# Retention and gated feed-forward on one core: two chunks' small products put in joint runs in two more places

## The chip, the core and the metric

The kernel runs on one core of a Trainium2 chip, as one program. The metric is device time in microseconds (us). Before the change three runs took 613.05, 612.64 and 612.45 us, a median of 612.64. The profiled execution that all views below come from took 613.15 us; its span from the first to the last instruction is 611.4 us, and the granted TensorE clock is 1.000 over the whole of it.

## The reference

The first half is a retention layer (batch 4, 8 heads, 768 steps, head size 64). The second half is a feed-forward layer over the 3072 resulting rows, with w_in of 512 x 2048 and w_out of 2048 x 512:

```python
for t in range(S):
    state = gamma * state + k_t (outer) v_t
    y[t] = scale * q_t @ state
x = y, as 3072 rows of 512
h = x @ w_in
sp = max(h, 0) + log1p(exp(-|h|))
out = (h * erf(sp)) @ w_out
```

## The kernel before, in words

**Chunks and groups.** The 3072 rows are 24 chunks of 128 steps (six for each batch entry). Two chunks, called a and b below, are a group of 256 rows; there are NG = 12 groups, numbered from 0. The retention of a chunk is computed in half-chunks of 64 steps, in products of 64 x 64 on quarters of TensorE's array, and gives the transposed input x of the feed-forward layer. The group's hidden values h = x @ w_in are computed 128 features at a time ("ft", 16 of them), go to DRAM, and are read back later for softplus, erf, the gate, and the product with w_out.

**The steps of one chunk j.**
- `ret_transpose(j)` (L447, called `T`): for the first six chunks, 4 + 4 transposes of keys and queries on TensorE (128 x 128, L453), copied out of PSUM by ScalarE (L459). Later chunks get theirs from VectorE (`prepare`, L531).
- `scale_early(j, 1)` and `scale_early(j, 0)` (L742): ScalarE scales the queries, then the values, by the decays, eight activations each (L746).
- `begin(j)` (L560): the scores of both half-chunks (L566) and what they add to the state (L573), 64 x 64 products into two PSUM banks.
- `states(j)` (L578): VectorE masks the scores into the tile `am` (L582) and adds up the states (L593).
- `results(j)` (L595): the products with the state (L611) and with the masked scores (L622), into two more banks; ScalarE copies them to x (L630).
- `crossed_sums(j)` (L633) adds a part of the results on VectorE (L641); `split_x` (L643) splits x into the parts hi, lo and dif that the three-product scheme uses (L314 to L316).

The last chunk of a batch entry has one half-chunk less to add to the state, and the first has no state for its first half.

**What sets the order.** The order on every engine is written out by hand: each engine works its queue in the order in which the Python code issues instructions. Three stretches matter here.

*First stretch, groups 0 to 2.* A loop over the 16 ft computes `hidden_of(ft, 0)` and `hidden_of(ft, 1)` (L659, plain f32 products, L665), and after each ft runs the steps that the table `during` (L799) lists for it, then `put_hidden(ft)` (L671): ScalarE copies the two groups' hidden values out of one of two PSUM buffers (L673), and GpSimd's queue stores them (L675). VectorE converts the 64-bit weights to f32 meanwhile (`conversion`, L237, lines L244 to L265), piece by piece, before the ft that needs them. The two chunks of the third group (4 and 5) are worked in here.

*Middle, `period(g)` (L936).* Eight `unit`s or `pair_unit`s (L687, L712) for each group, each 12 products of three-part f32 (L720), beside the chunks of group g + 1. For the groups 3 to 9 `joined(2, 5, g)` (L925) places `begin` of both chunks ahead of unit 2 and `results` of both ahead of unit 5, one right after the other.

*Last group but one, `period(10)`.* `begin(a)` stands ahead of unit 1, `results(a)` ahead of unit 2, `begin(b)` ahead of unit 3, `results(b)` ahead of unit 5. The units of this period go on to load and split w_out, and to start the first softplus.

**Buffers.** `b4` gives one of 34 SBUF buffers of 4 KB a partition, `b2` one of 6 of half that size. The tile `am` of a chunk (masked scores) is a `b2`; so is the tile h of `put_hidden` and of `put`, which is free again only when its store has landed. PSUM tiles come from the pools `ps_r` (2 banks), `ps_h` (2) and the four named banks o0 to o3.

**Tables.** `load_block_scales` (L387) loads small decay tables through GpSimd's queue in the first stretch; `block_scales` (L400) takes their reciprocals on VectorE (L401 to L403) and has GpSimd multiply them up (L405); the first reader is `prepare` of chunk 6 (L538).

Of the kernel before, what the change touches and what calls it, by code (L numbers as in the profile page):

```python
# [23 lines left out]
JPC = 4  # L24
# [25 lines left out]
def kernel(  # L50
# [14 lines left out]
    B, H, S, D = q.shape  # L65
    d_model, d_ff = w_in.shape
    HP = H // 2
# [17 lines left out]
    ps_r = ctx.enter_context(tc.tile_pool(name="ps_r", bufs=2, space=PSUM))  # L85
# [4 lines left out]
    def b4(name, shape, dtype=F32):  # L90
        return big.tile([P] + shape, dtype, name=name, tag="b4")

    def b2(name, shape, dtype=F32):
        return small.tile([P] + shape, dtype, name=name, tag="b2")
# [16 lines left out]
    KN, QN, V, KB, QB, KT, QT, SC, AM, SU = {}, {}, {}, {}, {}, {}, {}, {}, {}, {}  # L111
# [33 lines left out]
    def load_pair(j):  # L145

        b, c = divmod(j, NC)
        KNP[j] = b4("kn", [2, H, D])
        KB[j], QB[j] = (b4(name, [HP, 2 * C]) for name in ("kb", "qb"))
        for i in range(2):  # L150
            load_values(j + i, nc.gpsimd)
            KN[j + i], SLOT[j + i] = KNP[j][:, i], head
            nc.gpsimd.dma_start(KN[j + i], of_chunk(k, j + i))
        yield
        for to, src in ((KB[j], k), (QB[j], q)):
            for s, d in itertools.product(range(2), range(2)):
                part = slice((2 * s + d) * 32, (2 * s + d + 1) * 32)
                for u in range(HP):
                    nc.sync.dma_start(
                        to[part, u].rearrange("p (a d) -> p a d", d=32),  # L160
                        src[b, head(u, s), c * C : (c + 2) * C, d * 32 : (d + 1) * 32].rearrange(
                            "(a p) d -> p a d", p=32
                        ),
                    )
                yield
# [387 lines left out]
    def state_of(j, a):  # L553

        return None if j % NC == 0 and a == 0 else ST[(2 * j + a) % 5]

    def additions(j):
        return range(2 if j % NC < NC - 1 else 1)
# [18 lines left out]

    def states(j):  # L578

        AM[j] = b2("am", [2, HP, D])  # L580
        for s in range(2):
            nc.vector.tensor_tensor(  # L582
                AM[j][:, s],
                SC[j][s][:, :, :D],
                causal_d[:, None, :].to_broadcast([P, HP, D]),
                op=ALU.mult,
            )
        for a in additions(j):
            to, x, new = ST[(2 * j + a + 1) % 5], state_of(j, a), SC[j][a][:, :, D:]
            if x is None:  # L590
                nc.vector.tensor_copy(to, new)
            else:
                nc.vector.tensor_tensor(to, x, new, op=ALU.add)  # L593
# [118 lines left out]
    def pair_unit(g, ft):  # L712
# [23 lines left out]
    Q_, V_, T, S_, M, O_, A = (  # L736
        scale_q, scale_v, ret_transpose, ret_scores, ret_mask, ret_out, ret_add
    )
# [53 lines left out]
    def steps(s, n=1):  # L792
# [3 lines left out]
    pair = load_pair(JPC + 2)  # L796
    prep = prepare(JPC + 2)
    a, b = JPC, JPC + 1
# [1 line left out]
        1: [(load_block_scales,)],  # L800
        2: [(scale_early, a, 1), (steps, pair, 2)],
        3: [(scale_early, a, 0), (T, a, None, ("o2", "o3")), (steps, pair, 2)],
        4: [(begin, a, ps_r), (steps, pair, 2)],
        5: [(scale_early, b, 1), (states, a), (steps, pair, 2)],
        6: [(scale_early, b, 0), (results, a, ("o0", "o1")), (T, b, None, ("o2", "o3")), (steps, pair), (block_scales,)],
        7: [(crossed_sums, a), (begin, b, ps_r), (split_weights, 0)],
        8: [(states, b), (split_weights, 1)],
        9: [(results, b, ("o0", "o1"))],
        10: [(crossed_sums, b), (split_x, a, 2)],
        11: [(steps, prep, 3)],  # L810
        12: [(split_weights, 2), (steps, prep, 1)],
        13: [(steps, prep, 1)],
        14: [(begin, a + 2, ps_r), (begin, b + 2, None, ("o2", "o3")), (split_weights, 3), (states, a + 2), (states, b + 2)],
    }
    for ft in range(n_ft):
# [109 lines left out]
    def joined(at, to, g):  # L925

        a, b = 2 * g + 2, 2 * g + 3
        return {
            at: [(begin, a, ps_h), (begin, b, ps_r)],
            to: [(results, a, None, ps_h), (results, b, None, ps_r)],  # L930
        }
# [4 lines left out]
    def period(g, prep, next_prep):  # L936

        a, b = 2 * g + 2, 2 * g + 3
        one, two = partial(partial, unit), partial(partial, pair_unit)
        if g == G2:  # L940
            units = [one(g, n) for n in range(NPC // 2)]
            return units, {0: [(results, a), (results, b, None, ps_h)]}, {
                0: [(crossed_sums, a), (crossed_sums, b)],
                1: [(split_x, a, 2)],
                2: [(split_weights, 4)],
                3: [(steps, next_prep, 4)],
            }, range(4)
        if g < NG:
            units = [two(g - 1, ft) for ft in range(8 * (g % 2), 8 * (g % 2) + 8)]
        if g == G2 + 1:  # L950
            return units, joined(2, 5, g), {
                0: [(steps, prep)],
                1: [(split_weights, 5)],
                2: [(states, a), (states, b)],
                3: [(split_weights, 6)],
                4: [(split_weights, 7)],
                5: [(crossed_sums, a), (crossed_sums, b)],
                6: [(split_x, a, 2)],
                7: [(steps, next_prep, 1)],
            }, range(4)  # L960
        if g < NG - 2:
            return units, joined(2, 5, g), {
                0: [(steps, prep, 4)],
                1: [(convert, 2)],
                2: [(states, a), (convert, 1)],
                3: [(states, b), (convert, 1)],
                4: [(convert, 2 if g < 8 else 1)],
                5: [(crossed_sums, a), (crossed_sums, b)],
                6: [(split_x, a, 2)],
                7: [(steps, next_prep, 1 if g < NG - 3 else 4), (convert, 1)],  # L970
            }, LOADS.get(g, ())
        if g == NG - 2:
            return units, {1: [(begin, a)], 2: [(results, a)], 3: [(begin, b)], 5: [(results, b)]}, {
                0: [(steps, prep, 4), (load_w_out, 0)],
                1: [(states, a), (load_w_out, 1)],
                2: [(crossed_sums, a), (split_w_out, 0)],
                3: [(states, b), (split_x, a)],
                4: [(split_w_out, 1), (load_hiddens, 0)],
                5: [(crossed_sums, b)],
                6: [(split_x, b), (softplus, 0), (load_w_out, 2)],  # L980
                7: [(erf, 0), (gated, 0)],
            }, ()
        if g == NG - 1:
            return units, {}, {
                0: [(split_g, 0), (split_w_out, 2), (load_w_out, 3)],
                1: [(split_g, 1), (load_hiddens, 1)],
                2: [(split_w_out, 3)],
                3: [(softplus, 1), (load_w_out, 4)],
                4: [(erf, 1)],
                5: [(split_w_out, 4), (load_w_out, 5)],  # L990
                6: [(gated, 1)],
                7: [(split_g, 2), (load_hiddens, 2)],
            }, ()
        return [one(NG - 1, n) for n in range(NPC // 2)], {}, {
            0: [(split_w_out, 5), (load_w_out, 6)],
            1: [(split_g, 3), (load_w_out, 7)],
            2: [(split_w_out, 6)],
        }, ()

    for g in range(G2, NG + 1):  # L1000
        pair = load_pair(2 * g + 4) if 2 * g + 4 < NJ else iter(())
        next_prep = prepare(2 * g + 4) if 2 * g + 4 < NJ else iter(())
        units, pe, other, loads = period(g, prep, next_prep)
        for i, work in enumerate(units):
            for f, *args in pe.get(i, ()):
                f(*args)
            put = work()
            steps(pair, 3)
            for part in itertools.islice(quarters, loads.count(i)):
                load_quarter(part)  # L1010
            if g == NG - 1 and i % 2:
                W.pop(NPC // 2 + i // 2)
            if g == NG:
                W.pop(i)
            for f, *args in other.get(i, ()):
                f(*args)
            put()
            while behind:
                behind.pop(0)()
        prep = next_prep  # L1020
    split_w_out(7)

    for n in range(NG * NU):
        g, i = divmod(n, NU)
# [62 lines left out]
```

## Time and profile before

| | |
|---|---|
| runs, median | 613.05, 612.64, 612.45: 612.64 us |
| profiled execution, its span | 613.15 us, 611.4 us |
| TensorE (PE) busy | 604.6 us, 99% of the span |
| VectorE (DVE) busy | 459.8 us, 75% |
| ScalarE (ACT) busy | 390.3 us, 64% |
| GpSimd (POOL) busy | 132.5 us, 22% |
| granted TensorE clock | 1.000 |

Busy shares are averages over stages with different limits, so they say little about one place. More is read from the chain of work that ended last: from the last instruction back, each step's start is followed to whatever released it. Where the chain stays on one engine, that engine's queue sets the time, and each row of the chain (start, duration, engine, tile, line, number of instructions) is time that the program would be shorter by, were the row gone. The timeline gives the same kind of row for one engine, with its idle time ahead of it. A plain f32 product leaves two matmul records (32 for 16 products); a transpose and a product of the three-part scheme leave one.

### The profile page before, as it was taken

The page shows a single profiled execution, that of the slowest core. Times are in us where ns is not written, and L with a number is a line of the kernel's source. Part 1 is how long each engine was busy: PE and PEld are TensorE (multiplying, and loading weights), DVE is VectorE, ACT ScalarE, POOL GpSimd, SP SyncE. Part 2 cuts the span into 40 slices and gives each one's busy share as a digit, 9 for nine tenths or more (in the row PEclk, how much of TensorE's full clock was granted, in tenths as well). Part 3 has the DMA queues.
Part 4 walks back from the last instruction along what each step waited for, and adds up shares of the span by engine and source line. Part 5 has one row for each costly group of instructions (what it writes and reads, how often), then busy time and mean ns, then how long its engine had stood idle before and what let it go on. Part 6 is the DMA issues. An engine that isn't in the chain of part 4 may idle for free.

```text
span 611.4 us, 13214 instructions
## 1 busy us (share of the span) xinstructions
PE 604.6 (99%) x5222; PEld 507.3 (83%) x5222; DVE 459.8 (75%) x581; ACT 390.3 (64%) x614; POOL 132.5 (22%) x228
## 2 busy tenths in 40 slices
PE   8999999999999999999999999999999999999997
PEld 7888889888888888888788988888888888888886
DVE  5899988886978679787768978686776768668640
ACT  3667446354453634345387699889789888988920
POOL 1087435443526535241112200000000000000000
PEclk9999999999999999999999999999999999999999
DMA  9999659977979998894645834325324333531300
GB/s 203 312 263 281 149 132 248 265 161 221 219 201 277 269 270 182 243 233 151 215 143 187 286 119 148 127 70 173 103 88 154 106 129 110 172 119 55 103 35 34
DMA packets 143949, 106.28 MB, mean 174 GB/s; under 512 B 103056, under 2 KB 123792, under 8 KB 143888
## 3 DMA queue, kind: packets, MB, share of 16 engines
q1 hardware_dynamic: 128160, 58.09, 37.4%
q0 software_dynamic: 15168, 47.21, 24.6%
q8 instruction: 41, 0.67, 0.5%
q10 hardware_dynamic: 560, 0.14, 0.1%
q14 instruction: 20, 0.16, 0.1%
HBM read 69.75 MB, written 35.65 MB: 172 GB/s over the span
## 4 chain that ended last, share of the span: by engine, by line
PE 96%; SPq 2%; DMA 1%; ACT 0%; DVE 0%; issue 0%; DVEq 0%
PE o L720 31%; PE o L905 21%; PE r L905 11%; PE hp L905 11%; PE hp L665 9%; PE o L693 3%; PE hp L566 1%; DMA raw<-in_moe_w_in_dram 1%; PE hp L720 1%; PE r L720 1%; PE r L566 1%; PE r L611 1%; SPq L136 1%; PE r L622 1%; PE r L573 1%; PE hp L611 1%
## 5 line engine op out<-in xcount | busy, mean ns | idle before, releaser
L720 PE MATMUL o<-x_hi,w_hi 128*128 128x512 f32 x272 | 108.0, 397 | 0.0
L322 ACT ACTIVATE h<-o 128x512 f32<-128x512 f32 x74 | 43.8, 595 | 98.7 <-PE o L720 89.3
L720 PE MATMUL o<-x_lo,w_lo 128*128 128x512 f32 x272 | 106.0, 390 | 0.0
L860 DVE TENSOR_TENSOR e<-hid,e 128x1024 f32<-128x1024 f32 x48 | 56.7, 1222 | 61.9 <-ACT e L850 61.9
L323 DVE SCALAR_TENSOR_TENSOR h<-o,h 128x512 f32<-128x512 f32 x74 | 50.5, 686 | 34.3 <-ACT h L322 24.8
L720 PE MATMUL o<-x_dif,w_dif 128*128 128x512 f32 x272 | 72.7, 389 | 0.0
L731 POOL DMA_DIRECT2D hids<-h x72 | 39.6, 550 | 131.2 <-DVE h L323 123.1
L316 DVE SCALAR_TENSOR_TENSOR g_dif<-g_hi,g_lo 128x1024 fp32r<-128x1024 f32 x48 | 58.8, 1226 | 3.3
L720 PEld LDWEIGHTS o<-x_hi,w_hi 128*128 128x128 f32 x272 | 51.0, 188 | 11.4
L720 PEld LDWEIGHTS o<-x_dif,w_dif 128*128 128x128 f32 x272 | 51.1, 188 | 10.6
L314 ACT ACTIVATE g_hi<-e 128x1024 fp32r<-128x1024 f32 x48 | 51.0, 1062 | 13.5 <-DVE e L860 11.6
L720 PEld LDWEIGHTS o<-x_lo,w_lo 128*128 128x128 f32 x272 | 51.1, 188 | 10.1
L315 DVE TENSOR_TENSOR g_lo<-e,g_hi 128x1024 fp32r<-128x1024 f32 x48 | 58.6, 1221 | 0.5
L665 PE MATMUL hp<-xT,w 128*128 128x256 f32 x256 | 57.2, 381 | 0.0
L665 PEld LDWEIGHTS hp<-xT,w 128*128 128x128 f32 x256 | 48.0, 190 | 6.6
L846 ACT ACTIVATE e<-hid 128x1024 f32<-128x1024 f32 x48 | 48.2, 1052 | 0.3
L850 ACT ACTIVATE e<-e 128x1024 f32<-128x1024 f32 x48 | 48.2, 1052 | 0.3
L905 PE MATMUL o<-w_hi,g_hi 128*128 128x512 f32 x120 | 46.7, 389 | 0.0
L905 PE MATMUL o<-w_lo,g_lo 128*128 128x512 f32 x120 | 46.7, 389 | 0.0
L905 PE MATMUL o<-w_dif,g_dif 128*128 128x512 f32 x120 | 46.7, 389 | 0.0
L550 ACT ACTIVATE v<-v,kq_s 128x64 f32<-128x64 f32 x144 | 35.6, 335 | 0.0
L846 ACT ACT_TABLE_LOAD x24 | 30.8, 1283 | 0.5
(201 smaller groups left out, 1265.6 us busy)
## 6 DMA issues: line engine op xcount, KB each, us to landing
hids<-h POOLq DMA_DIRECT2D x72, 256.0 KB, 4.1
hid<-hids SPq DMA_DIRECT2D x36, 512.0 KB, 4.6
raw<-in_moe_w_in_dram SPq DMA_DIRECT2D x32, 256.0 KB, 5.5
raw<-in_moe_w_out_dram POOLq DMA_DIRECT2D x32, 256.0 KB, 6.2
hid<-hid SPq DMA_DIRECT2D x12, 512.0 KB, 5.2
out_dram<-y SPq DMA_DIRECT2D x23, 256.0 KB, 2.1
kb<-in_k_dram SPq DMA_DIRECT2D x144, 32.0 KB, 2.8
v<-in_v_dram POOLq DMA_DIRECT2D x18, 256.0 KB, 6.0
```

The lines of the kernel that those rows point to most:

```text
L314: nc.scalar.activation(hi, x, AF.Copy, scale=KEEP)
L315: nc.vector.tensor_tensor(lo, x, hi.bitcast(F32), op=ALU.subtract)
L316: nc.vector.scalar_tensor_tensor(dif, hi.bitcast(F32), Z, lo.bitcast(F32), op0=ALU.mult, op1=ALU.subtract)
L322: nc.scalar.activation(to, a, AF.Copy, scale=1 + 1 / Z)
L323: nc.vector.scalar_tensor_tensor(to, b, -1 / Z, to, op0=ALU.mult, op1=ALU.add)
L665: nc.tensor.matmul(HP_[ft][:, g], w[:, kk, ft % 2 * P : (ft % 2 + 1) * P], XC[g][:, kk], start=(kk == 0), stop=(kk == n_k - 1),)
L720: nc.tensor.matmul(to, W[n][i][:, kk * 2 * P + u * P : kk * 2 * P + (u + 1) * P], XR[i][:, at, kk], start=(kk == 0 and i == parts[0]), sto ...
L731: nc.gpsimd.dma_start(HID2[g][:, ft % 8], h)
L846: nc.scalar.activation(E[n], HID_[n], AF.Softplus)
L850: nc.scalar.activation(E[n], E[n], AF.Erf)
L860: nc.vector.tensor_tensor(E[n], HID_.pop(n), E[n], op=ALU.mult)
L905: nc.tensor.matmul(Y[g][t][x // 2], G[n][x][:, f, t * P : (t + 1) * P], W_OUT[ft // 2][x][:, ft % 2 * d_model : (ft % 2 + 1) * d_model], s ...
```

## The change

Three things are changed. In the third group's stretch, the transposes of chunk b come at ft 5 instead of ft 6, both `begin`s stand together at ft 6, and both `results` together at ft 9 (those of b now in `ps_r` instead of o0 and o1); the scalings of chunk b come one ft earlier. For that group both chunks' `am` are halves of one `b4` buffer. The reciprocals of the decay tables are taken at ft 8 instead of ft 6. In the last group but one, the hand-written table is replaced by `joined(1, 3, g)`: both `begin`s ahead of unit 1, both `results` ahead of unit 3; `states` of a and b follow in units 1 and 2, both `crossed_sums` in unit 3, and one `split_x` of both chunks in unit 5.

```diff
     def states(j):
-        AM[j] = b2("am", [2, HP, D])
+        if j == JPC:
+            both = b4("am", [2, 2, HP, D])
+            AM[j], AM[j + 1] = both[:, 0], both[:, 1]
+        elif j != JPC + 1:
+            AM[j] = b2("am", [2, HP, D])
...
         3: [(scale_early, a, 0), (T, a, None, ("o2", "o3")), (steps, pair, 2)],
-        4: [(begin, a, ps_r), (steps, pair, 2)],
-        5: [(scale_early, b, 1), (states, a), (steps, pair, 2)],
-        6: [(scale_early, b, 0), (results, a, ("o0", "o1")), (T, b, None, ("o2", "o3")), (steps, pair), (block_scales,)],
-        7: [(crossed_sums, a), (begin, b, ps_r), (split_weights, 0)],
-        8: [(states, b), (split_weights, 1)],
-        9: [(results, b, ("o0", "o1"))],
-        10: [(crossed_sums, b), (split_x, a, 2)],
+        4: [(scale_early, b, 1), (steps, pair, 2)],
+        5: [(scale_early, b, 0), (T, b, None, ("o0", "o1")), (steps, pair, 2)],
+        6: [(begin, a, ps_r), (begin, b, None, ("o2", "o3")), (steps, pair)],
+        7: [(states, a), (split_weights, 0)],
+        8: [(states, b), (split_weights, 1), (block_scales,)],
+        9: [(results, a, ("o0", "o1")), (results, b)],
+        10: [(crossed_sums, a), (crossed_sums, b), (split_x, a, 2)],
...
         if g == NG - 2:
-            return units, {1: [(begin, a)], 2: [(results, a)], 3: [(begin, b)], 5: [(results, b)]}, {
+            return units, joined(1, 3, g), {
                 0: [(steps, prep, 4), (load_w_out, 0)],
                 1: [(states, a), (load_w_out, 1)],
-                2: [(crossed_sums, a), (split_w_out, 0)],
-                3: [(states, b), (split_x, a)],
+                2: [(states, b), (split_w_out, 0)],
+                3: [(crossed_sums, a), (crossed_sums, b)],
                 4: [(split_w_out, 1), (load_hiddens, 0)],
-                5: [(crossed_sums, b)],
-                6: [(split_x, b), (softplus, 0), (load_w_out, 2)],
+                5: [(split_x, a, 2)],
+                6: [(softplus, 0), (load_w_out, 2)],
                 7: [(erf, 0), (gated, 0)],
```

## The prediction, as put on record before the changed kernel ran

> **What bounds the kernel now.** I read the engines' busy times first, then the chain of work that ended last. The page of the profiled run has
>
> ```profile
> PE 604.6 (99%) x5222; PEld 507.3 (83%) x5222; DVE 459.8 (75%) x581; ACT 390.3 (64%) x614; POOL 132.5 (22%) x228
> PE 96%; SPq 2%; DMA 1%; ACT 0%; DVE 0%; issue 0%; DVEq 0%
> ```
>
> TensorE is busy for 99% and the chain lies on it for 96%; the rest is the first loads. In both stretches of the change (36 to 92 us, 270 to 316 us) TensorE's busy time equals the stretch and its granted clock is 1.00. So TensorE waits for nobody there, and the change can win only what its own rows get shorter by. The chain, third group's stretch (start, us, tile, line, count):
>
> ```profile
> 38.55 0.87 PE o L453 x8
> 39.42 3.46 PE hp L665 x16
> 42.88 0.62 PE r L566 x32
> 43.50 0.47 PE r L573 x32
> 43.97 7.11 PE hp L665 x32
> 51.07 0.62 PE o L611 x32
> 51.70 0.47 PE o L622 x32
> 52.16 1.02 PE o L453 x8
> 53.19 3.46 PE hp L665 x16
> ```
>
> Three prices stand in it. Changing from large products to a run of small ones costs 0.15: the first 32 records take 0.62, the next 32 take 0.47. Changing back costs 0.19: two ft take 7.11 after a run, and 2 x 3.46 = 6.92 after transposes, which are large too and cost nothing on return (3.46). Transposes behind a run pay the same 0.15: 1.02 against 0.87.
>
> The chain around the last group but one, first a joint run of the period before, then separate ones:
>
> ```profile
> 275.74 0.62 PE hp L611 x32
> 276.37 0.47 PE hp L622 x32
> 276.83 0.49 PE r L611 x32
> 277.32 0.47 PE r L622 x32
> 277.79 11.11 PE o L720 x48
> 288.90 0.62 PE hp L566 x32
> 289.52 0.47 PE hp L573 x32
> 289.99 2.95 PE o L720 x12
> 292.94 0.62 PE r L611 x32
> ...
> 315.93 2.72 PE hp L720 x12
> ```
>
> In a joint run the second chunk starts at 0.49 (L611; 0.47 for L566 elsewhere) instead of 0.62. After any run, single or joint, the next unit costs 0.23 more: 2.95 against 2.72, and 11.11 against 4 x 2.72 = 10.88. So a joint run does not pay its saving back on its return.
>
> **The change, part by part.**
>
> *Third group, TensorE.* Before, from T(a) at 38.55 to the next run at 83.39: 0.87 + 3.46 + 1.09 + 7.11 + 1.09 + 1.02 + 3.46 + 1.08 + 7.11 + 1.09 + 17.46 = 44.84. After: T(a) 0.87, two ft 6.92, T(b) between large products 0.87, one ft 3.46, both begins 0.62 + 0.47 + 0.47 + 0.46 = 2.02, three ft 10.38 + 0.19 = 10.57, both results 0.62 + 0.47 + 0.49 + 0.47 = 2.05, five ft 17.46; together 44.22. **Gain 0.62**: one return 0.19, entries 0.15, 0.13 and 0.15.
>
> *Last group but one, TensorE.* Before, 277.79 to 313.21: 35.42. After: 11.11, begins 2.02, two units 5.44 + 0.23, results 2.05, five units 13.60 + 0.23; together 34.68. **Gain 0.74**: two returns of 0.23, entries 0.15 and 0.13.
>
> [...]
>
> *ScalarE, first stretch (cover to be checked).* Its queue gets chunk b's scalings one ft earlier. The timeline has
>
> ```profile
> 42.73 1.15 ACT L233 ACTIVATE power<-power,below 128x1024 uint32<-128x1024 uint32 x1 [0.52 <-DVE power L230]
> 43.78 0.56 ACT L673 COPY h<-hp 128x512 f32<-128x512 f32 x1
> 47.53 2.01 ACT L746 ACTIVATE kq<-kq,kq_s 128x64 f32<-128x64 f32 x8
> ```
>
> Now the query scaling stands ahead of that copy: 43.78 + 1.92 = 45.7, copy of ft 4 done at 46.2. TensorE needs that PSUM buffer for ft 6 at 47.21: 1.0 to spare. The queries were issued at 36.9 and 37.4 and land in 5.6, at 43.0: in time. Then L233 (to 47.5), the value scaling to 49.5 (values issued 39.01, landed after 6.5, at 45.5), T(b)'s copies to 50.5, ft 5's copy to 51.0. TensorE reaches begin(b) at 51.76 and ft 7 at 52.69: 1.2 and 1.7 to spare. T(b)'s keys land 5.9 after issue, by 44.4, needed at 46.34. Cost 0; without cover each us late beyond this is a us.
>
> *VectorE, first stretch.* Piece 5's conversion (4.95 from its rows) moves ahead, 48.77 to 53.7; states(a) (0.67 + 0.79, TensorE's part done by 51.8) to 55.2, first split 2.4 to 57.6, states(b) to 58.6, second split 61.0, reciprocals 0.6 to 61.7, piece 6 to 66.4. results(b) starts at 64.3: 5.7 to spare for states(b). Piece 5 is read at ft 10 (65.3), piece 6 at ft 12 (72.2). VectorE's waits of 0.67 (reciprocals for their loads) and 0.63 (masked scores of b for a `b2` whose store had not landed) go, and ScalarE's of 2.59 for an h buffer should. What is late next there is nothing: TensorE did not wait for them, so they count 0.
>
> *GpSimd, the tables.* L405 (5 in 1.55) moves behind the stores of ft 6 and 7 and now waits for the reciprocals at 61.7, done at 63.3. Queued behind it: the stores of ft 8 on, some 2.5 later than at 60.8; that h buffer is next wanted at ft 14, near 80, and the tables at 75.85 (L538). Cost 0. SP's loads keep their order; the `b4` more for `am` changes which freed buffer some later loads take, all freed long before.
>
> *Last group but one, the others.* On the old clock: begins 288.90 to 290.9, units 1 and 2 to 296.59, results. Chunk b's queries are transposed by 288.1 and its values scaled by 287.8. VectorE masks a by 291.7, waits for unit 1 (293.9), subtracts for 0.6 (L323), masks and adds b (0.66 + 0.41) by 295.6. results(b) starts at 297.7: 2.1 to spare. The w_out split (2.4) and L323 of unit 2 end near 298.6, before unit 4's second bank wants them (past 303). Sums of both chunks by 300, split of x (2.4) at unit 5 by 308; the first reader is period 11 at 312.5. Cost 0. All later stages are TensorE row by row and shift.
>
> **Sum:** 0.62 + 0.74 = 1.36. The profiled execution's 613.15 (span 611.4 and 1.75 around it) becomes 611.8; it is 0.5 above the median, and 612.64 becomes **611.3**, 0.22% less.
>
> **Rivals.**
> - *One stretch gives its gain back.* A cover of 1.0 (ScalarE's copy of ft 4) or 2.1 (masking of b) is smaller than it seems: other DMA timing, queue latency. Against it: the same joint form runs in seven periods with TensorE never idle; for it: there three units lie between, here two, and ScalarE is fuller at 42 to 51 us than elsewhere. Time 612.64 - 0.74 = 611.9, or - 0.62 = 612.0. Chance 0.22.
> - *Slower: chunk b's values land late.* They are now needed at 47.5 instead of 49.9, in the fullest DMA stretch, and T(b)'s copies and ft 5's queue behind them on ScalarE, so TensorE stops at begin(b). Landing later than 45.5 + 2.0 + 1.2 = 48.7 costs us for us; from 50.1 on the change loses. At twice the landing time (13.0, at 52.0) it is 3.3 - 1.36 = 1.9 slower: 614.6. Against it: 8.1 is the longest landing of such a load in the trace. Chance 0.05.
> - *A change of mode is worth less than the rows say*, because part of the 0.23 is only how ends of matmuls are drawn: half the price gives 612.0. Against it: the chain's starts, not ends, give the sums. [...]
>
> **How the numbers follow.** The forecast has 0.70, with 610.8 to 611.7 as its own range (three runs spread over 0.6). A measurement of this kernel can tell about 0.2%, 1.2 us, from no change; the forecast lies just past it, so of its 0.70 I count 0.57 as faster and 0.13 as within. Faster 0.57, within 0.2% 0.13 + 0.22 + 0.03 = 0.38, slower 0.05. Range 610.7 to 612.3: it takes in the forecast and the first and third rivals.
>
> **What would show it.** After: at some 50.6 us one run of 2.02 with a single 0.62, at 63.2 one of 2.05, T(b) at 0.87, and 17.46 starting 0.62 earlier; near 288 and 295 joint runs, and the first unit on `r` 1.36 earlier than 313.21. Wrong would be idle time or weight-load waits on TensorE ahead of ft 6, begin(b), ft 7 (ScalarE), or the second results (VectorE), and a first row above 0.62 or returns above 0.23.

## The result and the profile after

The changed kernel takes 611.54 us (median of 15 runs, 611.12 to 612.7) and the kernel before, in 15 runs beside it, 612.83 (612.45 to 614.45). The ratio is 0.9978, with a 95% interval of 0.9971 to 0.9985: 1.35 us less, or between 0.9 and 1.8. The forecast of 611.3 stood on a gain of 1.36. The profiled execution has a span of 609.6 us, against 611.4 before; 0.4 of these 1.8 comes ahead of all that was changed (T(a) starts at 38.11 instead of 38.55).

Behind line 581 all lines stand four higher than before: L611 is now L615, L622 is L626, L665 is L669, L673 is L677, L720 is L724, L746 is L750.

From the profile page of the changed kernel, the engines' busy times, and the shares of the chain of work that ended last:

```profile
PE 603.3 (99%) x5222; PEld 507.3 (83%) x5222; DVE 459.4 (75%) x579; ACT 390.1 (64%) x613; POOL 135.2 (22%) x228
PE 97%; DMA 1%; SPq 1%; DVE 0%; issue 0%; ACT 0%; DVEq 0%
```

TensorE has the same 5222 records, busy for 1.3 us less: the same work got shorter. It is still at 99%, and the chain lies on it for 97%. GpSimd's 2.7 us more come up at the end.

The chain of work that ended last, third group's stretch of the changed kernel (start, us, tile, line, count):

```profile
38.11 0.87 PE o L453 x8
38.99 6.91 PE hp L669 x32
45.90 0.87 PE o L453 x8
46.77 3.46 PE hp L669 x16
50.23 0.62 PE r L566 x32
50.85 0.47 PE r L573 x32
51.32 0.47 PE o L566 x32
51.78 0.46 PE o L573 x16
52.24 10.56 PE hp L669 x48
62.80 0.62 PE o L615 x32
...
64.83 17.46 PE hp L669 x80
82.29 0.62 PE r L566 x32
```

Each piece begins where the last one ends, so TensorE waits for nobody. There is one 0.62 ahead of each joint run where there were two; T(b) takes 0.87 between large products, where it took 1.02; three ft take 10.56 in one piece, with one return. From T(a) to the next run it is 82.29 - 38.11 = 44.18. Before, that run started here:

```profile
83.39 0.62 PE r L566 x32
```

So before it was 83.39 - 38.55 = 44.84, and the forecast was 44.22. Gain 0.66.

The same chain, last group but one of the changed kernel:

```profile
276.74 11.10 PE o L724 x48
287.84 0.62 PE hp L566 x32
...
289.86 5.67 PE o L724 x24
295.53 0.62 PE hp L615 x32
...
297.58 13.82 PE o L724 x60
311.40 2.72 PE r L724 x12
```

Two units in one piece take 5.67 = 2 x 2.72 + 0.23, the five after the results 13.82 = 5 x 2.72 + 0.22. From 276.74 to 311.40 it is 34.66. Before, the first unit on `r` started here:

```profile
313.21 2.72 PE r L720 x12
```

So before it was 313.21 - 277.79 = 35.42, and the forecast was 34.68. Gain 0.76, and 1.42 with the first, beside 1.35 from the runs.

### The profile page after: what moved, and what is told of

The parts are those of the page before. It is cut to its first block, busy times and chain, and to the rows that moved or that the text cites. A ratio compares the mean times of both kernels' runs of the same rounds, so it can differ in the third digit from the quotient of the medians.

```text
span 609.6 us, 13214 instructions
## 1 busy us (share of the span) xinstructions
PE 603.3 (99%) x5222; PEld 507.3 (83%) x5222; DVE 459.4 (75%) x579; ACT 390.1 (64%) x613; POOL 135.2 (22%) x228
## 4 chain that ended last, share of the span: by engine, by line
PE 97%; DMA 1%; SPq 1%; DVE 0%; issue 0%; ACT 0%; DVEq 0%
PE o L724 31%; PE o L909 21%; PE r L909 11%; PE hp L909 11%; PE hp L669 9%; PE o L697 3%; PE hp L724 1%; PE r L724 1%; PE hp L615 1%; PE hp L566 1%; PE r L566 1%; DMA q<-in_q_dram 1%; PE r L615 1%; PE r L626 1%; PE r L573 1%; PE hp L626 1%
## 5 line engine op out<-in xcount | busy, mean ns | idle before, releaser
L724 PE MATMUL o<-x_hi,w_hi 128*128 128x512 f32 x272 | 107.8, 396 | 0.0
L724 PE MATMUL o<-x_lo,w_lo 128*128 128x512 f32 x272 | 106.0, 390 | 0.0
L724 PE MATMUL o<-x_dif,w_dif 128*128 128x512 f32 x272 | 72.7, 389 | 0.0
L724 PEld LDWEIGHTS o<-x_hi,w_hi 128*128 128x128 f32 x272 | 51.0, 188 | 11.3
L724 PEld LDWEIGHTS o<-x_dif,w_dif 128*128 128x128 f32 x272 | 51.1, 188 | 10.6
L724 PEld LDWEIGHTS o<-x_lo,w_lo 128*128 128x128 f32 x272 | 51.1, 188 | 10.1
L315 DVE TENSOR_TENSOR g_lo<-e,g_hi 128x1024 fp32r<-128x1024 f32 x48 | 58.6, 1221 | 0.8 <-ACT g_hi L314 0.3
L669 PE MATMUL hp<-xT,w 128*128 128x256 f32 x256 | 56.9, 381 | 0.0
L669 PEld LDWEIGHTS hp<-xT,w 128*128 128x128 f32 x256 | 48.1, 190 | 6.6
```

What stands on the lines that cost most here:

```text
L315: nc.vector.tensor_tensor(lo, x, hi.bitcast(F32), op=ALU.subtract)
L669: nc.tensor.matmul(HP_[ft][:, g], w[:, kk, ft % 2 * P : (ft % 2 + 1) * P], XC[g][:, kk], start=(kk == 0), stop=(kk == n_k - 1),)
L724: nc.tensor.matmul(to, W[n][i][:, kk * 2 * P + u * P : kk * 2 * P + (u + 1) * P], XR[i][:, at, kk], start=(kk == 0 and i == parts[0]), sto ...
```

## Experiments

The theory: TensorE is the bound in both stretches, and the change wins what its rows of entering and leaving runs of small products get shorter by, because no cover is used up. Rivals: a cover fails in one stretch, an edit that I counted at nothing is worth something, or the rows of the chain draw the price wrongly.

**Each stretch alone.** The first kernel has the third group's part with the last group but one as before; the second has the reverse.

```diff
 # e1_third_group
-            return units, joined(1, 3, g), {
+            return units, {1: [(begin, a)], 2: [(results, a)], 3: [(begin, b)], 5: [(results, b)]}, {
 # e2_last_but_one: rows 4 to 10 of `during` and `states` as before the change
```

> The third group's part alone; the last group but one keeps its separate runs. Theory (each run of small products costs a fixed price for going in and coming back, and nothing else of the change counts): 0.62 less than before by the rows of before, in the chain 44.2 from the transposes of a to the next run instead of 44.84, and 35.4 for the last group but one; about 612.2 where before has 612.8, ratio 0.9990. Rival (the whole gain comes from the waits that the buffer and the later reciprocals take off VectorE and ScalarE in this stretch): 1.35 less, 611.5, ratio 0.9978.

> The last group but one alone; the third group, its buffer and its reciprocals stay as before. Theory (fixed price for each run of small products): 0.74 less, 34.7 instead of 35.42 in the chain from the last units of the period before to the first unit on r, about 612.1, ratio 0.9988. Rival (the gain is all in the third group's stretch): nothing, ratio 1.0000.

Measured: 612.26 and 612.17 beside 612.86 before, both 0.9989 (0.9981 to 0.9998), some 0.7 us each. The traces divide it more sharply than the times can. With the third group's part alone the first stretch goes from 38.28 to 82.46, 44.18, and the second from 276.93 to 312.39, 35.46, where before had 35.42. With the other part alone it is 44.84 as before and 277.81 to 312.48, 34.67. So each part brings what its rows say, and they add up.

**The big buffer and the later reciprocals.** The two side edits taken back together, then one at a time. They change nothing in TensorE's order, and I had counted them at 0.

```diff
 # e3_old_buffers and e8_small_scores
-        if j == JPC:
-            both = b4("am", [2, 2, HP, D])
-            AM[j], AM[j + 1] = both[:, 0], both[:, 1]
-        elif j != JPC + 1:
-            AM[j] = b2("am", [2, HP, D])
+        AM[j] = b2("am", [2, HP, D])
 # e3_old_buffers and e9_tables_early
-        6: [(begin, a, ps_r), (begin, b, None, ("o2", "o3")), (steps, pair)],
+        6: [(begin, a, ps_r), (begin, b, None, ("o2", "o3")), (steps, pair), (block_scales,)],
-        8: [(states, b), (split_weights, 1), (block_scales,)],
+        8: [(states, b), (split_weights, 1)],
```

> Both joins as in the changed kernel, but the masked scores in the small buffers again and the reciprocals at ft 6 again. Theory: VectorE waits for the tables there (some 2 us from 48.5, until they have landed near 50.7) and everything behind them on it moves later, but the masked scores of b are still ready near 60, ahead of the second results at 63.9; TensorE row by row the same as in the changed kernel, ratio 0.998. Rival (the buffer and the later reciprocals carry the gain, or the join needs them): TensorE shows idle time ahead of the third group's results, 0.5 us or more given back, ratio 0.9987 or above.

> The changed kernel with only the masked scores back in the small buffers; the reciprocals stay late. Theory (the buffer is the part that the join needs: with it taken, the copy of ft 7's hidden values gets the buffer of ft 2, whose store lands near 59.8 here, while TensorE wants ft 9's bank at 59.1): TensorE idle ahead of ft 9 for about 1.3, as with both parts undone, ratio to before 0.9996. Rival (what gave the gain back was VectorE's wait for the tables): nothing lost, ratio 0.998.

> The changed kernel with only the reciprocals back at ft 6; the masked scores stay in the big buffer. Theory (the buffer is what the join needs): VectorE waits 2 us for the tables and TensorE does not notice, ratio 0.998; GpSimd's five products of L405 run at another place. Rival (the tables): about 1.2 us given back, ratio 0.9996.

Measured, beside 612.86 before for the first kernel and 612.8 for the other two: both back 612.69, 0.9996 (0.9987 to 1.0005); only the buffer back 612.72, 1.0000 (0.9992 to 1.0009); only the reciprocals back 611.50, 0.9978 (0.9969 to 0.9987). The buffer decides, and taking it back costs 1.2 us, nearly the whole gain. So the expectation for both back (nothing lost) missed, and its rival held. The reciprocals' place is worth nothing that these runs can tell.

The timeline of the kernel with only the buffer back, TensorE and VectorE (start, us, what, in brackets the idle time ahead of it and who ended it; L665 is the large product here):

```profile
52.29 7.17 PE L665 MATMUL hp<-xT,w 128*128 128x256 f32 x32
60.21 3.72 PE L665 MATMUL hp<-xT,w 128*128 128x256 f32 x16 [0.74 <-ACT h L673]
60.30 0.75 DVE L582 TENSOR_TENSOR am<-o,causal_d 128x256 f32<-128x256 f32 x2 [2.70 <-DMA hid<-h]
```

The three ft fall apart: after two of them TensorE is idle for 0.74 (some 1.3 had been expected), and the third takes 3.72 for 3.46. Together 7.17 + 0.74 + 3.72 = 11.63 instead of the changed kernel's 10.63 in the same view. TensorE waits for ScalarE's copy of ft 7. The copy's row in this kernel, and then in the kernel with both edits back:

```profile
59.57 0.58 ACT L673 COPY h<-hp 128x512 f32<-128x512 f32 x1 [6.08 <-PE hp L665]
```

```profile
59.86 0.58 ACT L673 COPY h<-hp 128x512 f32<-128x512 f32 x1 [4.26 <-DMA hid<-h]
```

With both back ScalarE sat idle for 4.26 until a store had landed. The copy's target h is a `b2`, and there are six; with `am` in two of them the copy waits for the store of ft 2, issued at 51.06 and landed at 59.76, 8.7 us later. With only the buffer back the row names TensorE's products (L665), but those of ft 7 had ended near 56.0; the products that ended at 59.48 are those of ft 8, which this copy does not read. The store of ft 2 landed near 59.5 by my estimate: the copy's start at 59.57 less the 0.10 that lie between landing and copy with both back. VectorE's masking waits 2.70 for another such store. Before the change such waits were there too (2.59 and 0.63) and cost nothing; the section on the prediction says why they do now.

**The price of a change, made larger.** In the periods 4 to 9 each joint run is taken apart into two, twelve more trips in and out.

```diff
 # e4_all_apart
-            return units, joined(2, 5, g), {
+            return units, {2: [(begin, a, ps_h)], 3: [(begin, b, ps_r)], 4: [(results, a, None, ps_h)], 5: [(results, b, None, ps_r)]}, {
-                4: [(convert, 2 if g < 8 else 1)],
-                5: [(crossed_sums, a), (crossed_sums, b)],
+                4: [(crossed_sums, a), (convert, 2 if g < 8 else 1)],
+                5: [(crossed_sums, b)],
```

> The changed kernel with the joint runs of the groups 4 to 9 taken apart: begin of a ahead of unit 2, of b ahead of unit 3, results of a ahead of unit 4, of b ahead of unit 5. Theory (fixed price): two returns of 0.23 and entries of 0.15 and 0.13 more in each of six periods, 6 x 0.74 = 4.4 us more than the changed kernel, near 615.9, ratio to before 1.005. Rival (the price is special to the two stretches that the change touched): no more than 1 us, 612.5, ratio 0.9995.

Measured: 615.82, 1.0048 (1.0034 to 1.0062), 4.3 us above the changed kernel. The chain of this kernel, two results of one group:

```profile
141.52 0.63 PE hp L615 x32
142.14 0.47 PE hp L626 x32
142.61 2.95 PE o L724 x12
145.56 0.62 PE r L615 x32
```

Now b's results pay an entry of their own (0.62), and the unit between pays a return (2.95 for 2.72). Twelve times 0.13 to 0.15 of entry and 0.23 of return is 4.3 to 4.6. The price holds in a measured time, so it is no matter of how ends of products are drawn.

**One product between large ones.** To see what of the price is the change of size, one product of 64 columns is put ahead of four units in each of the periods 4 to 10, 28 in all: of 64 x 64, of 128 x 128 in plain f32, and of 128 x 128 in the three-part format of its neighbours. Its result is used by nothing and overwritten at once.

```diff
+        if 3 <= g < NG - 2 and ft % 8 in (0, 3, 6, 7):
 # e5_one_small
+            one = ident[:64, :64]
+            nc.tensor.matmul(a.rearrange("p g t -> p (g t)")[:64, :64], one, ident[:64, :64], start=True, stop=True)
 # e6_one_large: the same with 128 for each of the first two 64
 # e10_one_three_part
+            nc.tensor.matmul(
+                a.rearrange("p g t -> p (g t)")[:, :64],
+                W[n][0][:, u * P : (u + 1) * P], XR[0][:, at.start, 0, :64], start=True, stop=True,
+            )
```

> The changed kernel with one more 64 x 64 product of 64 columns (identity times identity, overwritten at once by the unit) ahead of four units in each of seven periods; 27 of the 28 stand between large products, one directly behind a run. Its results are used by nothing. Theory (the price is for the change between large and small products, in and out, whatever the run's length): 0.15 + 0.23 and the product itself, 0.05 to 0.12 by the rows of the runs, 27 times: 11.6 to 13.5 us more than the changed kernel, near 624, ratio to before 1.018. Rival (the price comes from the run's length, from weight loads that could not run ahead during 64 or 128 small records): only the product itself, 28 x 0.05 to 0.12 = 1.4 to 3.4, near 614, ratio 1.002.

> The same 28 places with one plain f32 product of 128 x 128 and 64 columns instead, so the number format changes and the size on the array does not. Its results are used by nothing. Theory (the price is for the size on the array): the product alone, a quarter of the 0.43 that 256 columns take in the f32 products of the first stretch, 28 x 0.11 = 3.0 us more than the changed kernel, near 614.5, ratio 1.003. Rival (what costs in the middle is the change between plain f32 and the three-part format): 0.23 to 0.38 more at each place, 9.5 to 13.7, near 623, ratio 1.016.

> The changed kernel with, in the same 28 places as the lone small and lone large products, one product of 128 x 128 and 64 columns in the units' own three-part format; its result is overwritten at once. Neither size nor format changes there. Theory (the 0.14 beyond its own time that a lone plain f32 product costs is the weight load that a short product cannot hide): its own time, an eighth of 0.227, or 0.03, and the same 0.14, 28 x 0.17 = 4.8 more than the changed kernel, near 616.3, ratio 1.006. Rival (the 0.14 is the change of number format): 28 x 0.03 = 0.8 more, near 612.3, ratio 0.999.

Measured: 64 x 64 takes 624.52, 1.0186 (1.0169 to 1.0203), 12.9 above the changed kernel; large plain f32 618.71, 1.0094 (1.0079 to 1.0109), 7.1 above; the large one in the format of its neighbours 615.22, 1.0039 (1.0023 to 1.0054), 3.7 above. The chains of the three, first 64 x 64:

```profile
149.95 0.26 PE o L724 x2
150.20 2.94 PE o L727 x12
```

then the large one in plain f32:

```profile
149.04 0.17 PE o L724 x2
149.21 2.80 PE o L727 x12
```

and the large one in the format of its neighbours:

```profile
148.82 0.03 PE o L723
148.85 2.83 PE o L729 x12
```

The first row of each is the extra product (plain f32 is two records), the second the unit behind it, of 2.72 otherwise. A trip costs 0.26 + 0.22 = 0.48, 0.17 + 0.08 = 0.25, and 0.03 + 0.11 = 0.14; 27 x 0.48 = 13.0 (the one small product directly behind a run shows 0.07 only), 28 x 0.25 = 7.0 and 28 x 0.14 = 3.9 are within 0.2 of the measured times. For the large f32 product both numbers on record missed (3.0 and 9.5 to 13.7), and for the one in the format of its neighbours the theory's 4.8 came nearer than the rival's 0.8. So the change of size by itself is some 0.48 - 0.25 = 0.23 for a trip of one product, if the small and the large f32 product take the same time by themselves. Of the slower unit behind a run (0.22) a third to a half (0.08 and 0.11) comes behind a single large product of 64 columns too, with no change of size. Where these 0.08 and 0.11 come from is not shown, nor is the weight load that the theory names for them.

**A late cover.** The second rival said that what comes late on ScalarE ahead of T(b)'s copies costs us for us beyond 1.2. Here ScalarE copies chunk b's values onto themselves six times ahead of them, or four times.

```diff
+    def linger(n):
+        x = V[b].rearrange("p h d -> p (h d)")
+        for _ in range(2 * n):
+            nc.scalar.copy(x, x)
 # e7_linger; e11_linger_less has (linger, 2)
-        5: [(scale_early, b, 0), (T, b, None, ("o0", "o1")), (steps, pair, 2)],
+        5: [(scale_early, b, 0), (linger, 3), (T, b, None, ("o0", "o1")), (steps, pair, 2)],
```

> The changed kernel with six copies of chunk b's values onto themselves (128 x 512, about 0.5 each, 3.0 to 3.6 in all) on ScalarE ahead of the copies of b's transposes. Theory (the first stretch is covered by about 1.1 us there): the transposes are copied out at 53.2 to 53.8 instead of 50.1, TensorE is idle ahead of begin of b, which it reaches at 51.3, for 1.9 to 2.5 us, and the time is that much longer, near 613.7, ratio 1.0015. Rival (cover is ample, TensorE has other work to hide it): nothing, ratio 0.998.

> The changed kernel with four instead of six copies of chunk b's values onto themselves ahead of the copies of b's transposes, 2.6 by the 0.65 that one took with six. Theory (1.1 of cover, and the lower clock after the wait of 2.7 with six copies was worth another 1.7): TensorE idle ahead of begin of b for 1.5, the granted clock stays at 1.00 as after the wait of 1.3 with the old buffers, 1.5 more than the changed kernel, near 613.0, ratio 1.0003. Rival (any wait over a microsecond brings the lower clock): 1.5 + 1.7 = 3.2 more, near 614.7, ratio 1.003.

Measured: six copies 616.14 (614.29 to 616.63), 1.0046 (1.003 to 1.0062), 4.5 above the changed kernel; four copies 613.82 (612.89 to 615.49), 1.0018 (1.0007 to 1.0028), 2.3 above. The copies took 3.87 and 2.57. The timeline of the kernel with six, TensorE at begin(b):

```profile
54.62 0.69 PE L566 MATMUL o<-kqT 64*64 64x64 f32 x32 [2.72 <-ACT kqT L459]
```

With four the same row stands at 53.87 with 1.45. Both are the copies' time less the cover: 3.87 - 2.72 = 1.15, 2.57 - 1.45 = 1.12, where the prediction had 1.2. But a wait of 2.72 should have cost 2.7, not 4.5: the expectation of 613.7 for six copies missed. The busy time by stretches of 1 us of the kernel with six copies has the rest (behind the engines, the granted clock, then DMA share and GB/s):

```profile
55.60:56.60 1.00, 1.00 (x10) 0.79 (x7) 0.00 (x0) 1.00 (x2) 0.00 (x0) 0.86 1.05 186
...
57.60:58.60 1.00, 1.00 (x4) 0.82 (x3) 1.00 (x1) 0.00 (x0) 0.55 (x2) 0.50 1.04 362
...
59.60:60.60 1.00, 1.00 (x6) 0.90 (x5) 1.00 (x3) 0.00 (x0) 0.76 (x2) 0.94 1.09 303
```

The granted clock fell to 0.50 at about 56.3, 1.7 after TensorE had resumed, and was back at 59.7, 3.4 later; the three ft took 12.24 for 10.56, 1.7 lost. 2.7 + 1.7 = 4.4 is about the measured loss. The single executions say the same: of the four with six copies three have a mean clock of 0.997 and took 616.05 to 616.63, and one has 1.000 and took 614.29, 2.75 above the changed kernel. Of the ten with four copies, four have 0.997 and took 614.6 to 615.5; six have 0.999 or 1.000 and took 612.9 to 614.2, four of them 612.9, 1.4 above, which is the wait of 1.45 us for us. So with four copies neither text on record holds for all: 613.0 fits the ones at full clock, 614.7 the lowest of the others. (The execution with the profile, 614.21 at 0.999, has 1.1 more from the first loads: TensorE's first large product behind them, L669, starts at 22.93 instead of 21.82. The one at 613.42 and 1.000 has no trace.)

## Why the prediction was right

- **What bounds the kernel, and the three prices.** Right. Each term came within 0.02 (two ft 6.91 for 6.92, begins 2.01 for 2.02, three ft 10.56 for 10.57, two units 5.67, five 13.82 for 13.83), 44.18 for 44.22 and 34.66 for 34.68. The runs apart (e4) and the single products (e5) show the price in measured times. The rival that had the price of a change of mode (between large and small products) at half, a gain of 0.68 with a chance of 0.03, lies just outside the measured 0.9 to 1.8, and e4 excludes it more clearly, 4.3 where it would give 2.2.
- **ScalarE's covers.** Right. Ft 4's copy ended at 45.86, and ft 6 began at 46.77: 0.9 to spare for a forecast of 1.0. (One reading was off without effect: in the kernel before, T(b)'s keys landed at 44.54, not by 44.4; they were needed at 46.34.) T(b)'s copies ended at 50.2, begin(b) came at 51.32, and the two kernels that linger put this cover at 1.12 to 1.15.
- **VectorE's covers.** Right. In the first stretch states(b) was done at 58.6 and wanted at 63.9, 5.3 to spare for a forecast of 5.7; in the last group but one it was done at 294.6 and wanted at 296.62, 2.0 to spare for a forecast of 2.1.
- **One stretch gives its gain back.** Did not happen: e1 and e2 show both gains.
- **Slower: chunk b's values late.** Did not happen: they landed at 44.90, and their scaling began at 47.29. The price, us for us, was too low: behind the wait of 2.72 the clock fell as well, for 1.7 more. And 8.1 is not the longest landing of such a load in the trace of the kernel before: one issued at 186.2 took 9.2.
- **"What is late next there is nothing: TensorE did not wait for them, so they count 0."** Against the kernel before this is true, and it is where the working was too quick. I took the waits of 0.63 and 2.59 as harmless because they were harmless before, and so the bigger buffer as an edit without effect. With joint runs they are not: ft 9 starts at 59.2 in the changed kernel instead of 61.2, in the main since the results of a no longer stand ahead of it, while the store that frees ft 7's target still lands at 59.76 (e3) or, by my estimate, near 59.5 (e8). Without the big buffer the third group's part loses 1.0 in the stretch (7.17 + 0.74 + 3.72 for 10.63) and 1.2 in the time, more than the 0.66 it wins. The term was 0 in the sum only since the buffer came with the change.
- **"(5 in 1.55)" on GpSimd.** Mis-sized: 4.68. The stores behind it were issued from 66.2 instead of 63.3. It still cost nothing, with their buffer wanted near 80.
- **The tables' reciprocals later.** Counted at 0, and no cost shows (e9: 44.17 from T(a) to the next run, for 44.18).

## What to carry to other kernels

When one engine is the bound and its chain has no gaps, a reordering can be priced from the chain's rows, entry and return by entry and return; here each term came within 0.02 us. A wait that costs nothing before a change has a margin that depends on when the bound engine comes; work it out again in the new order, since here the wait on ScalarE that was harmless before (2.59) would have taken nearly the whole gain back (1.2 of 1.35, e8). An added wait on TensorE should not always be priced us for us: here one of 2.72 cost about 4.4, as the clock fell behind it.

## What the runs showed of the hardware

**The clock behind a short wait.** TensorE idle for 2.72 us, and soon after, the granted clock at 0.50 for 3.4 us; idle for 1.29 (both edits back) and 1.45 (the profiled execution with four copies), and it stayed at 1.00. In four of ten executions with four copies the mean clock fell by the same 0.003 as with six. If their wait was that of the profiled execution, one near 1.4 can be enough; none of the four has a trace. In the 22 executions of the two kernels with `am` in the small buffers (0.74 and 1.29 of idle time in the profiled ones) the mean clock was never below 0.999. Why executions of one kernel differ is not shown.

**The same five products of GpSimd, three times as long.** The timeline of the changed kernel:

```profile
61.58 4.68 POOL L405 TENSOR_TENSOR kq_b<-kq_b,by_b 128x32 f32<-128x32 f32 x5
```

Before, the same five took 1.55 from 59.00. VectorE was busy for 4.61 of the 4.68 here and for 0.92 of the 1.55 there. In the kernels of the experiments it goes the same way: 1.53 with VectorE busy for 0.90 of it (e3), 3.84 with 3.81 (e1). A median product takes 0.242 before and 1.101 after. Spans on GpSimd are rough, but this is a factor of three. One product of the five, and what VectorE does meanwhile:

```profile
63.90 1.10 POOL L405 TENSOR_TENSOR kq_b<-kq_b,by_b 128x32 f32<-128x32 f32 x1
63.65 1.26 DVE L253 SCALAR_TENSOR_TENSOR power<-raw,power 128x1024 uint32<-128x1024 uint32 x1
```

The product ends at 65.00, 0.09 behind VectorE's instruction, which reads two tensors in SBUF. Each of the five ends 0.09 to 0.10 behind the end of a VectorE instruction. Those instructions are L244, L249, L230, L253 and L265; L244 and L230 read one tensor only, the others two. Before, four of the five took 0.24 each, while VectorE was idle or worked on the masked scores and the state (L582, L593), with one input in PSUM. What holds the products up is not shown.
